# Order of the first loads and of the last units in a kernel of windowed attention and a gated MLP

## The chip, the cores and the metric

The kernel runs on one core of one Trainium2 chip. The time is that of the device in microseconds (us); shown is the median of several executions. One execution was also taken by the hardware profiler, and all times of single instructions are from it. The engines are named as in the profile: PE (TensorE, matmul), PEld (its weight loads), DVE (VectorE), ACT (ScalarE), POOL (GpSimd), and SP (SyncE, which issues most transfers). An engine works through its own instructions in the order in which they stand.

## The reference: what is computed

A sequence of 2048 rows of 512 numbers, x, is normalized to xn. One branch (A) is attention with 32 heads of 16 numbers over a window of 8 rows at distance 2; the other (B) is a layer norm, a mixing of neighbouring rows, and an MLP. Their product is added to x:

```python
xn = _layernorm(x, axis=-1)
s = _A_ref(xn, A_wqkv, A_wo)
g = _silu(_B_ref(xn, B_w1, B_w2, B_w3, B_w4))
return x + s * g
```

with, in short,

```python
# A: q, k, v from xn @ wqkv, heads of 16, row i sees rows i, i-2, ..., i-14
logits = jnp.einsum("bhsd,bhswd->bhsw", q, kg) * scale
...
o = jnp.einsum("bhsw,bhswd->bhsd", attn, vg)
return (lambda x, *d: x.transpose(*d))(o, 0, 2, 1, 3).reshape(B, S, D) @ wo
# B
h = _gelu(_layernorm(x, axis=-1) @ w1)
...
x1 = x + hs
h2 = _gelu(_layernorm(x1, axis=-1) @ w3) @ w4
return x1 + h2
```

## The kernel before, in words

**Tiling.** Since the window steps by two rows, even and odd rows never meet in the attention; the rows are split by parity p (0, 1), 1024 rows each. A tile of x is 128 rows of 512 numbers of one parity (bf16, 128 KB); four tiles make a chunk c (chunks 0 and 1 are parity 0, chunks 2 and 3 parity 1), and x tile j of chunk c is found by `x_tile(c, j)`. All data stay on the chip in arrays `xn`, `xnT` (turned), `kT`, `qT`, `oT`.

**Start.** SP issues the loads in the order of the code (lines 115 to 133): tiles 0 and 1 of chunk 0, the first half of the q/k weights as one transfer of 512 KB (`wqk_sb[:, :, 0:512]`, the q columns), tiles 2 and 3, the second half (the k columns), then chunks 1 and 2 in pairs of tiles, `w1`, and chunk 3. PE meanwhile makes ten matmuls on ones (L147). For tiles 0 and 1 DVE takes statistics (`stats`, L208 and L209), ACT the root (`root`, L217), DVE the inverse and the norm (L220, L224). `first_columns` (L290 to L293) turns both tiles on PE and copies half of the result by DVE and half by ACT. Then the same statistics, roots and norms follow for tiles 2 and 3 (lines 438 to 443). `qk(0, 0)` (L309) makes 32 matmuls of 256 columns for the first two tiles, in groups nt 0 to 7: groups 0 to 3 use the first half of the weights and 4 to 7 the second, and ahead of groups 6 and 7 PE turns tiles 2 and 3 (L264).

**Middle.** qk, w1, w2, w3 for all chunks. Each of these runs on PE with little else in its way.

**Units.** The attention goes in 17 units n (0 to 16; `NN = 17`): unit 0 holds the first rows of both parities, units 1 to 8 are parity 0, 9 to 16 parity 1, 120 query rows each. One turn n of the loop (lines 868 to 929) has the scores of unit n (L616), the weighted sum of unit n - 1 (L663), ACT's exp (L627), the values of the next unit (L595), one tile of the MLP's w4 product (L542), DVE's band mask (`within`, L636), and an output tile (`final`, L815). The weighted sum lies in `o_ps` and is taken out by DVE (L679, L680) and ACT (`evict`, L681) to `orw`; from there small transfers (`moves`, L706, one for each of 8 head groups) put the rows into `oT`. The softmax denominators of a run of units are gathered, inverted, written to DRAM and read back (L692, L770, L772, L778), and the result is multiplied into `oT` (`sums_apply`, L786). The last three runs (units 14, 15, 16; `R - 3` to `R - 1`) do this without DRAM: `sums_turn` (L716, PE), `sums_inverse` (L724 DVE; L729 ACT spreads the inverse over 16 columns), `sums_back` (L754, PE), `sums_mult` (L763, DVE). Units 15 and 16 also come to `oT` by `rows` (L741 PE, L746 ACT) and not by transfers.

**Output.** `final(p, i)` makes tile i of parity p: four matmuls with `wo`; then `gate(eng)`: DVE multiplies with the gate (L826, or L824 where the gate came by silu), and `eng` (mostly POOL) adds x (L831). `store` (L857) writes two tiles at a time. The gate of tile t is x1 + h2 (`w4_part`, DVE add at L550) through a tanh form of silu (L568, L574); for t = 14 and 15 (`NN - 3`, `NN - 2`) ACT's own silu is used (`gate_silu`, L560), for which L935 loads its table. For t = 15 PE adds x by an identity matmul (L548) and silu reads the matmul's result.

**What sets the order.** At the end (lines 977 to 984) every engine's instructions are tied to the order of the code. The order among the engines is found by a scheduler. It also hands out semaphores: transfers issued by SP and ACT get one of eight completion semaphores in turn, in the order in which the scheduler issues them.

Of the kernel before, what the change touches and what calls it, by code (L numbers as in the profile page):

```python
# [8 lines left out]
AF = mybir.ActivationFunctionType  # L9
ALU = mybir.AluOpType  # L10
# [5 lines left out]
def kernel(  # L16
# [68 lines left out]
    def smt(shape, name):  # L85
        return sm4.tile(shape, BF16, name=name, tag="s4")
# [25 lines left out]
    xn = [bigt([P, M // P, D], f"xn{p}") for p in range(2)]  # L112
    wqkv_v = A_wqkv.rearrange("(dt q) n -> q dt n", q=P)

    def load_x(c, n):
        p, k = c // 2, c % 2
        for t0 in range(k * TPC, (k + 1) * TPC, n):
            sp.dma_start(
                out=xn[p][:, t0 : t0 + n, :],
                in_=xv[p, t0 * P : (t0 + n) * P, :].rearrange("(i q) d -> q i d", q=P),  # L120
            )
            yield

    wqk_sb = midt([P, ND, 2 * D], "wqk_sb")
    first = load_x(0, 1)
    for k in range(2):
        next(first), next(first)
        sp.dma_start(out=wqk_sb[:, :, k * D : (k + 1) * D], in_=wqkv_v[:, :, k * D : (k + 1) * D])
    list(load_x(1, 2))
    list(load_x(2, 2))  # L130
    w1_sb = smt([P, ND, D], "w1_sb")
    sp.dma_start(out=w1_sb, in_=B_w1.rearrange("(dt q) n -> q dt n", q=P))
    list(load_x(3, 2))

    act.preload_act_table_set("sqrt_and_others")
    ident = const.tile([P, P], BF16, name="ident")
# [63 lines left out]
    def x_tile(c, j):  # L200
        return xn[c // 2][:, (c % 2) * TPC + j, :]

    def stats(c, j, key="l1"):
        if (key, c) not in mvs:
            mvs[key, c] = small.tile([P, TPC, nc.vector.BN_AGGR_DIM], F32, name=key + "m", tag=key + "m")
            rs[key, c] = small.tile([P, TPC], F32, name=key + "r", tag=key + "r")
        st = small.tile([P, nc.vector.BN_STATS_DIM], F32, name=key + "s", tag=key + "s")
        dve.bn_stats(out=st, in_=x_tile(c, j))  # L208
        dve.bn_aggr(out=mvs[key, c][:, j, :], in_=st)  # L209
# [6 lines left out]
    def root(c, a, b):  # L216
        act.activation(rs["l1", c][:, a:b], mvs["l1", c][:, a:b, 1], AF.Sqrt, bias=eps[:, 0:1])  # L217
# [211 lines left out]

    stats(0, 0)  # L430
    root(0, 0, 1)
    stats(0, 1)
    root(0, 1, 2)
    for j in range(2):
        inverse(0, j, j + 1)
        norm(0, j)
# [98 lines left out]
    def w4_part(t, lo, hi, tag="w"):  # L535
        c, jj = t // TPC, t % TPC
        if lo == 0:
            banks["w4", t] = pst(tag, "w4_ps")[:, 0, :]
        pt = banks["w4", t]
        for ft in range(lo, hi):  # L540
            fs = P if ft < NF - 1 else FL
            pe.matmul(  # L542
                pt, lhsT=h3[c][:fs, ft, jj * P : (jj + 1) * P], rhs=w4_sb[:fs, ft, :],
                start=(ft == 0), stop=(ft == NF - 1 and t < NN - 2),
            )
        x_i = x_tile(c, jj)
        if hi == NF and t == NN - 2:
            pe.matmul(pt, lhsT=ident[:], rhs=x_i, start=False, stop=True)  # L548
        elif hi == NF:
            dve.tensor_tensor(out=x_i, in0=pt, in1=x_i, op=ALU.add)  # L550
            gates.append(t)


    gates = []
    twice = set()

    def gate_silu(t):

        x_i = x_tile(t // TPC, t % TPC)
        act.activation(x_i, banks["w4", t] if t == NN - 2 else x_i, AF.Silu)  # L560
        twice.add(t)

    def gate_tanh():
# [74 lines left out]
    orw = {}  # L638
# [77 lines left out]
            pe.matmul(pt[0:QU, g, :], lhsT=w[:, g, :], rhs=ident[:, DH::32], start=True, stop=True)  # L716
        rden[i] = pt

    def sums_inverse(i, copy=lambda: None, behind=False):

        pt = rden[i]
        rb = small.tile([P, 2 * ND, 4], BF16, name="rbt", tag="rbt")
        with nc.allow_low_precision("bf16 weights"):
            dve.reciprocal(out=rb[0:QU], in_=pt[0:QU])  # L724
        if not behind:
            copy()
        rx = slot().rearrange("p (s j c d) -> p s j c d", s=ND, j=2, c=4)
        for j in range(2):
            act.activation(  # L729
                rx[0:QU, :, j], rb[0:QU, j * ND : (j + 1) * ND, :].unsqueeze(3).to_broadcast([QU, ND, 4, DH]), AF.Copy  # L730
            )
        if behind:
            copy()
        rden[i] = rx

    def rows(i, tag):

        pt = pst(tag, "row_ps")[:, 0, 0 : ND * QU].rearrange("p (s q) -> p s q", s=ND)
        for dt in range(ND):
            for jj in range(2):  # L740
                pe.matmul(  # L741
                    pt[P // 2 * jj : P // 2 * (jj + 1), dt, :], lhsT=heads, rhs=orw[i][:, ND * jj + dt, :],
                    start=True, stop=True, tile_position=(0, P // 2 * jj),
                )
        _, _, _, q0, rw, parts = run_of(runs[i][0])
        return lambda: act.activation(oT[parts[0][0]][:, :, q0 : q0 + rw], pt, AF.Copy)  # L746

# [108 lines left out]
    def store(q, p, i, n=2, cs=slice(0, D)):  # L856
        q.dma_start(  # L857
            out=ov[p, i * P : (i + n) * P, cs].rearrange("(i q) d -> q i d", q=P),
            in_=xo[p, i & ~1][:, i % 2 : i % 2 + n, cs],
        )  # L860
# [7 lines left out]
    for n in range(NN - 1):  # L868
        scores(n)
        back = [i for i, (a, b) in enumerate(runs) if b == n - 2 and i < R - NC]  # L870
        done = [i for i, (a, b) in enumerate(runs) if b == n - 1]
        evict = weighted(n - 1) if n > 0 else lambda: None
        for i in back:
            sums_invert(i)
        exps(n, 2 if n == 0 else 1)
        if n == NN - 2:
            values(n + 1)
        evict()
        if 0 < n < NN - 2:
            values(n + 1)  # L880
        gate_mult()
        if n < NN - 2:
            gate_tanh()
        for i in done:
            if i < R - NC:
                sums_gather(i)
        if n == 2:
            moves(0, [sp, pool], 1)
        for i in back:
            if 0 < i < R - NC - 1:  # L890
                moves(i, [sp], None, [6, 7])
            sums_read(i)
        for i in done:
            if i == 0:
                moves(i, [sp, pool], 0)
            elif i < R - NC - 1:
                moves(i, [pool, sp], None, range(6))
            elif i == R - NC - 1:
                moves(i, [pool], None, range(4))
            else:  # L900
                moves(i, [pool, sp])
        if n == NN - 2:
            store(sp, 0, 6)
        within(n, 2 if n == 0 else 1)
        late = [i for i, (a, b) in enumerate(runs) if n == max(b + 3, 5)]
        w4_part(n, 0, NF if n < NN - 2 else CUT)
        if n == 0:
            values(n + 1)
        gate = final(*final_at[n]) if n in final_at else None
        if n == NN - 2:  # L910
            banks["end"] = True
            sums_turn(R - 3, "o")
            sums_inverse(R - 3)
            for i in late:
                sums_apply(i)
        if gate:
            gate(pool)
        if n < NN - 2:
            for i in late:
                sums_apply(i)  # L920
        if n == NN - 3:
            moves(R - NC - 1, [pool], None, range(4, 8))
        if n % 2 == 0 and 10 <= n < NN - 3:
            load_xo((n - 2) // 8, (n - 2) % 8)
        if n - 1 in final_at and n % 2 == 0 and n < NN - 3:
            p, i = final_at[n - 1]
            store(sp, p, i - 1)
        if n in (10, 12):
            load_xo(1, n - 6)
    scores(NN - 1)  # L930
    evict = weighted(NN - 2)
    store(sp, 1, 0)
    exps(NN - 1)
    evict()
    act.preload_act_table_set("silu_and_others")  # L935
    w4_part(NN - 2, CUT, NF)
    gate_silu(NN - 2)
    within(NN - 1)
    gate2 = final(1, 2, "b")
    layout("high", f=1, g=1, h=1, i=1)  # L940
    sums_back(R - 3, "f")
    gate3 = final(1, 3, "h")
    sums_apply(R - 4, pool)
    evict = weighted(NN - 1, first=lambda: gate2(pool))
    evict()
    sums_turn(R - 2, "g")
    sums_inverse(R - 2, rows(R - 2, "i"), True)
    gate3(pool)
    store(sp, 1, 2)
    gate4 = final(1, 4, "w")  # L950
    sums_mult(R - 3)
    sums_turn(R - 1, "g")
    sums_back(R - 2, "f")
    sums_inverse(R - 1, rows(R - 1, "h"), True)
    sums_mult(R - 2)
    gate_silu(NN - 3)
    gate5 = final(1, 5, "b")
    gate4(pool)
    gate5(pool)
    store(sp, 1, 4)  # L960
    sums_back(R - 1, "i")
    gate6 = final(1, 6, "g")
    sums_mult(R - 1)
    halves = [slice(0, D // 2), slice(D // 2, D)]
    add6 = pe_add(1, 6, "o", slice(0, D))
    gate6(None)
# [48 lines left out]
```

## Time and profile before

| what | us |
|---|---|
| median of 3 runs (lowest, highest) | 198.9 (197.78, 199.8) |
| the profiled execution | 197.92 |
| its span, first to last instruction | 195.9 |
| PE busy in the span | 189.5 |
| ACT busy | 126.7 |
| DVE busy | 124.1 |
| POOL busy | 62.9 |
| DMA bytes in the span | 23.36 MB |
| first matmul of qk starts at | 6.73 |
| last scores (unit 16) start at | 180.13 |
| last projection (rows of parity 1, tile 7) starts at | 190.81 |

How to read the lines: in a timeline a row is start, duration, engine, line of the code, operation, output and inputs with their sizes, how many, and in brackets how long the engine had been idle before and what ended the wait. SPq, ACTq and POOLq are the issue of transfers by that engine; the row's duration is that of the issue and not of the transfer.

### The profile page before, as it was taken

The numbers are of one execution on the slowest core, as the hardware profiler recorded it, in microseconds if no ns is written. First come the engines' busy times: TensorE is split into PE (matmuls) and PEld (weight loads), VectorE is DVE, ScalarE is ACT, GpSimd is POOL, SyncE is SP. The second block draws the span as 40 slices with busy tenths as digits, with TensorE's granted clock in tenths as the row PEclk, the third lists the DMA queues.
The fourth block names the chain that finished last, engine by engine and source line by source line (L and its number), as shares of the span: only waits on it lengthen the run. The fifth ranks groups of instructions, "written<-read, shape, count | busy, mean of one in ns | idle before, by whom it ended". The sixth has DMA issues, their size and how long they took to land.

```text
span 195.9 us, 6180 instructions
## 1 busy us (share of the span) xinstructions
PE 189.5 (97%) x2607; PEld 100.7 (51%) x2607; DVE 124.1 (63%) x247; ACT 126.7 (65%) x140; POOL 62.9 (32%) x114
## 2 busy tenths in 40 slices
PE   7799999999999999999999999999999999999992
PEld 2688748644444444444445555555555545546551
DVE  4879885029359968200005677788778888886893
ACT  3579867836721534666558788887666666677971
POOL 4146738201301121100000623032625242469761
PEclk9999999999999999999999999999999999999999
DMA  5985265799660366350420012222233271723243
GB/s 149 330 270 137 77 144 161 141 300 357 185 155 3 107 157 162 113 107 0 155 84 0 14 25 65 76 48 67 44 97 67 56 210 27 234 39 87 70 141 109
DMA packets 36251, 23.36 MB, mean 119 GB/s; under 512 B 19680, under 2 KB 35712, under 8 KB 36224
## 3 DMA queue, kind: packets, MB, share of 16 engines
q1 hardware_dynamic: 34864, 22.11, 40.2%
q0 software_dynamic: 1216, 0.81, 2.1%
q8 instruction: 20, 0.33, 0.7%
q10 hardware_dynamic: 144, 0.07, 0.1%
q14 instruction: 7, 0.06, 0.1%
HBM read 12.41 MB, written 5.36 MB: 91 GB/s over the span
## 4 chain that ended last, share of the span: by engine, by line
PE 90%; DVE 4%; ACT 2%; DMA 1%; issue 1%; DVEq 0%
PE w_ps L542 19%; PE w_ps L406 18%; PE qk_ps L309 14%; PE v_ps L595 8%; PE w_ps L342 7%; PE w_ps L366 7%; PE wo_ps L815 5%; PE o_ps L663 5%; PE s_ps L616 3%; PE w_ps L422 1%; DMA xn<-in_A_x_dram 1%; ACT prob L627 1%; DVE prob L636 1%; PE tr_ps L264 1%; PE dt_ps L716 1%
## 5 line engine op out<-in xcount | busy, mean ns | idle before, releaser
L627 ACT ACTIVATE prob<-s_ps 128x2048 bf16<-128x2048 f32 (+1 forms) x18 | 31.9, 1780 | 17.9 <-PE s_ps L616 17.9
L542 PE MATMUL w_ps<-w_sb,h3T 128*128 128x512 bf16 (+1 forms) x176 | 40.8, 380 | 0.0
L410 ACT ACTIVATE h3T<-w_ps 128x1024 bf16<-128x1024 f32 x20 | 20.5, 1023 | 24.9 <-PE w_ps L406 24.9
L706 POOL DMA_DIRECT2D oT<-orw x38 | 19.4, 518 | 49.8 <-DVE orw L671 30.3
L406 PE MATMUL w_ps<-x1nT,w_sb 128*128 128x512 bf16 x160 | 35.0, 379 | 0.0
L309 PE MATMUL qk_ps<-xnT,wqk_sb 128*128 128x256 bf16 (+1 forms) x224 | 29.7, 288 | 0.5 <-DVE xnT L292 0.4
L542 PEld LDWEIGHTS <-h3T 128*128 128x128 bf16 (+1 forms) x176 | 17.0, 98 | 20.4
L309 PEld LDWEIGHTS <-wqk_sb 128*128 128x128 bf16 x224 | 21.5, 98 | 7.6 <-issue 0.8
L406 PEld LDWEIGHTS <-w_sb 128*128 128x128 bf16 x160 | 15.6, 98 | 19.1 <-issue 0.4
L636 DVE TENSOR_TENSOR prob<-prob,band 128x2048 bf16<-128x2048 bf16 (+1 forms) x18 | 21.3, 1183 | 2.4 <-ACT prob L627 2.3
L316 ACT ACTIVATE qT<-qk_ps,sel 128x1024 bf16<-128x1024 f32 x16 | 16.8, 1111 | 7.1 <-PE qk_ps L309 7.0
L831 POOL TENSOR_TENSOR xo<-sg,xo 128x512 bf16<-128x512 bf16 x9 | 11.7, 1305 | 21.6 <-DVE sg L826 21.6
L371 DVE TENSOR_TENSOR xn<-w_ps,xn 128x1024 bf16<-128x1024 f32 x8 | 9.7, 1212 | 13.2 <-PE w_ps L366 13.2
L815 PE MATMUL wo_ps<-wo_sb,oT 128*128 128x512 bf16 (+1 forms) x68 | 16.6, 367 | 0.1
L595 PE MATMUL v_ps<-wv_sb,xnT 128*128 128x512 bf16 x64 | 16.6, 382 | 0.0
L550 DVE TENSOR_TENSOR xn<-w_ps,xn 128x512 bf16<-128x512 f32 x15 | 10.4, 690 | 7.5 <-PE w_ps L542 7.5
L598 DVE CAST v_aug<-v_ps 128x512 bf16<-128x512 f32 x1 | 0.7, 691 | 22.5 <-ACT h3T L410 22.5
L681 ACT ACTIVATE orw<-o_ps 128x896 bf16<-128x896 f32 x16 | 14.6, 913 | 0.4 <-PE dt_ps L716 0.4
L366 PE MATMUL w_ps<-w_sb,hT 128*128 128x512 bf16 x64 | 14.3, 379 | 0.0
L342 PE MATMUL w_ps<-xn2T,w_sb 128*128 128x512 bf16 x64 | 14.3, 379 | 0.0
L213 POOL TENSOR_SCALAR l3r<-l3m 128x4 f32<-128x4 f32 x4 | 1.8, 451 | 36.9 <-DVE l3m L209 36.9
L663 PE MATMUL o_ps<-prob,v_aug 64*32 64x64 bf16 x1088 | 12.2, 196 | 0.3 <-DVE prob L636 0.2
(100 smaller groups left out, 240.1 us busy)
## 6 DMA issues: line engine op xcount, KB each, us to landing
x1n_dram<-xn SPq DMA_DIRECT2D x4, 512.0 KB
xn<-in_A_x_dram SPq DMA_DIRECT2D x6, 256.0 KB
xo<-in_A_x_dram SPq DMA_DIRECT2D x6, 256.0 KB
out_dram<-xo SPq DMA_DIRECT2D x6, 256.0 KB
orw<-rden_d SPq DMA_DIRECT2D x6, 240.0 KB
w_sb<-in_B_w_dram SPq DMA_DIRECT2D x1, 1376.0 KB
w_sb<-in_B_w_dram SPq DMA_DIRECT2D x1, 1280.0 KB
wqk_sb<-in_A_wqkv_dram SPq DMA_DIRECT2D x2, 512.0 KB
```

Source lines behind the costliest of these rows:

```text
L309: pe.matmul(pt[:, b, :], lhsT=wqk_sb[:, dt, nt * P : (nt + 1) * P], rhs=xnT[p][:, dt, ms], start=(dt == 0), stop=(dt == ND - 1),)
L342: pe.matmul(pt[:, b, :], lhsT=w1_sb[:, dt, g * P : (g + 1) * P], rhs=xn2T[:, dt, :], start=(dt == 0), stop=(dt == ND - 1),)
L366: pe.matmul(pt[:, j, :], lhsT=w2_src(p, g, m0), rhs=w2_sb[:, g, :], start=(g == 0), stop=(g == ND - 1),)
L406: pe.matmul(pt[:, b, :], lhsT=w3_sb[:, dt, ft * P : (ft + 1) * P], rhs=x1nT[:, dt, :], start=(dt == 0), stop=(dt == ND - 1),)
L410: act.activation(h3_tile(c)[:, 2 * a : 2 * a + 2, :], pt, AF.Gelu_apprx_tanh)
L542: pe.matmul(pt, lhsT=h3[c][:fs, ft, jj * P : (jj + 1) * P], rhs=w4_sb[:fs, ft, :], start=(ft == 0), stop=(ft == NF - 1 and t < NN - 2),)
L595: pe.matmul(vp, lhsT=xnT[p][:, dt, k0 : k0 + P], rhs=wv_sb[:, dt, :], start=first, stop=last)
L627: act.activation(pr[:, rs_], t[:, rs_], AF.Exp, scale=SCALE)
L636: dve.tensor_tensor(out=w, in0=w, in1=b.unsqueeze(1).to_broadcast([P, m, KB]), op=ALU.min)
L663: pe.matmul(op[32 * cg : 32 * cg + 32, s, g * KB : (g + 1) * KB], lhsT=va[KB * s : KB * s + KB, dt * 8 + h, :], rhs=pr[KB * s : KB * s + K ...
L706: queues[hh % len(queues)].dma_start(out=oT[p][DH * hh : DH * (hh + 1), :, q0 : q0 + nq], in_=w[32 * cg : 32 * cg + DH, ND * jj : ND * jj ...
L815: pe.matmul(pt, lhsT=oT[p][:, dt, i * P : (i + 1) * P], rhs=wo_sb[:, dt, cs], start=(dt == 0), stop=(dt == ND - 1),)
```

## The change

At the start, `load_x` now loads n tiles from tile j on, on a queue that is given, and `load_qk(k)` loads half k of the q/k weights as four transfers of 128 KB, one for each 128 rows of the matrix. SP issues tiles 0 and 1 and the first half ahead of the rest; x tiles 2 and 3 are issued by ACT, one after each of the first two roots; SP's next ones in the code are the second half, chunks 1 and 2, w1, chunk 3.

At the end, for units 14 to 16 and their outputs: unit 14's eight moves go three to SP (issued ahead of the reading of unit 13's sums) and five to POOL, and not in turn to both; `sums_inverse` hands back its ACT part as `spread`, which is called later (for unit 14 after the exp of unit 16 and the eviction of unit 15); `gate(None)` multiplies tile (1, 1) ahead of `sums_apply`, and its add on POOL comes after unit 13's `sums_apply`; `w4_add` on DVE takes the place of the identity matmul for t = 15, whose silu moves behind that of t = 14; `sums_back` of unit 14 and the gates of tiles (1, 2), (1, 3) and (1, 4) change places; `rows` uses 2 matmuls of 480 columns where it had 8 of 120.

```diff
+    def load_x(c, j, n=1, queue=sp):
+        p, t0 = c // 2, c % 2 * TPC + j
+        queue.dma_start(
+            out=xn[p][:, t0 : t0 + n, :], in_=xv[p, t0 * P : (t0 + n) * P, :].rearrange("(i q) d -> q i d", q=P)
+        )
+
+    def load_qk(k):
+        for dt in range(ND):
+            sp.dma_start(out=wqk_sb[:, dt, k * D : (k + 1) * D], in_=wqkv_v[:, dt, k * D : (k + 1) * D])
...
-    first = load_x(0, 1)
-    for k in range(2):
-        next(first), next(first)
-        sp.dma_start(out=wqk_sb[:, :, k * D : (k + 1) * D], in_=wqkv_v[:, :, k * D : (k + 1) * D])
-    list(load_x(1, 2))
-    list(load_x(2, 2))
...
+    for j in range(2):
+        load_x(0, j)
+    load_qk(0)
...
     root(0, 0, 1)
+    load_x(0, 2, 1, act)
     stats(0, 1)
     root(0, 1, 2)
+    load_x(0, 3, 1, act)
+    load_qk(1)
+    for c in (1, 2, 3):
+        if c == 3:
+            w1_sb = smt([P, ND, D], "w1_sb")
+            sp.dma_start(out=w1_sb, in_=B_w1.rearrange("(dt q) n -> q dt n", q=P))
+        for j in (0, 2):
+            load_x(c, j, 2)
...
-        x_i = x_tile(c, jj)
-        if hi == NF and t == NN - 2:
-            pe.matmul(pt, lhsT=ident[:], rhs=x_i, start=False, stop=True)
-        elif hi == NF:
-            dve.tensor_tensor(out=x_i, in0=pt, in1=x_i, op=ALU.add)
-            gates.append(t)
+        if hi == NF and t < NN - 2:
+            w4_add(t)
...
-        for dt in range(ND):
-            for jj in range(2):
-                pe.matmul(
-                    pt[P // 2 * jj : P // 2 * (jj + 1), dt, :], lhsT=heads, rhs=orw[i][:, ND * jj + dt, :],
...
+        for jj in range(2):
+            pe.matmul(
+                pt[P // 2 * jj : P // 2 * (jj + 1)], lhsT=heads, rhs=orw[i][:, ND * jj : ND * (jj + 1), :],
...
+        if n == NN - 2:
+            moves(R - 3, [sp], None, range(3))
...
-                moves(i, [pool, sp])
+                moves(i, [pool], None, range(3, 8))
...
             sums_turn(R - 3, "o")
-            sums_inverse(R - 3)
+            spread14 = sums_inverse(R - 3)
+            gate(None)
             for i in late:
                 sums_apply(i)
-        if gate:
+        elif gate:
             gate(pool)
...
     evict = weighted(NN - 2)
-    store(sp, 1, 0)
     exps(NN - 1)
     evict()
+    spread14()
     act.preload_act_table_set("silu_and_others")
     w4_part(NN - 2, CUT, NF)
-    gate_silu(NN - 2)
     within(NN - 1)
+    w4_add(NN - 2)
     gate2 = final(1, 2, "b")
     layout("high", f=1, g=1, h=1, i=1)
-    sums_back(R - 3, "f")
     gate3 = final(1, 3, "h")
     sums_apply(R - 4, pool)
-    evict = weighted(NN - 1, first=lambda: gate2(pool))
+    gate.add(pool)
+    store(sp, 1, 0)
+    gate2(pool)
+    evict = weighted(NN - 1)
     evict()
     sums_turn(R - 2, "g")
-    sums_inverse(R - 2, rows(R - 2, "i"), True)
+    spread15 = sums_inverse(R - 2)
+    copy15 = rows(R - 2, "i")
+    sums_back(R - 3, "f")
     gate3(pool)
     store(sp, 1, 2)
+    spread15()
+    copy15()
     gate4 = final(1, 4, "w")
     sums_mult(R - 3)
+    gate4(pool)
     sums_turn(R - 1, "g")
     sums_back(R - 2, "f")
-    sums_inverse(R - 1, rows(R - 1, "h"), True)
+    spread16 = sums_inverse(R - 1)
+    copy16 = rows(R - 1, "h")
+    spread16()
+    copy16()
     sums_mult(R - 2)
     gate_silu(NN - 3)
+    gate_silu(NN - 2)
     gate5 = final(1, 5, "b")
-    gate4(pool)
     gate5(pool)
+    sums_back(R - 1, "i")
+    sums_mult(R - 1)
     store(sp, 1, 4)
-    sums_back(R - 1, "i")
     gate6 = final(1, 6, "g")
-    sums_mult(R - 1)
```

More of the change, by code (lines that the diff above doesn't have):

```diff
@@ L113 @@
     wqkv_v = A_wqkv.rearrange("(dt q) n -> q dt n", q=P)
[L115 to L122, printed above, removed]
-    wqk_sb = midt([P, ND, 2 * D], "wqk_sb")
-    first = load_x(0, 1)
-    for k in range(2):
-        next(first), next(first)
-        sp.dma_start(out=wqk_sb[:, :, k * D : (k + 1) * D], in_=wqkv_v[:, :, k * D : (k + 1) * D])
-    list(load_x(1, 2))
-    list(load_x(2, 2))
-    w1_sb = smt([P, ND, D], "w1_sb")
-    sp.dma_start(out=w1_sb, in_=B_w1.rearrange("(dt q) n -> q dt n", q=P))
-    list(load_x(3, 2))
+    def load_x(c, j, n=1, queue=sp):
[6 more added lines that the diff above has]
+            sp.dma_start(out=wqk_sb[:, dt, k * D : (k + 1) * D], in_=wqkv_v[:, dt, k * D : (k + 1) * D])
+    wqk_sb = midt([P, ND, 2 * D], "wqk_sb")
+    for j in range(2):
+        load_x(0, j)
+    load_qk(0)
     act.preload_act_table_set("sqrt_and_others")
@@ L543, in w4_part, with w4_add @@
                 pt, lhsT=h3[c][:fs, ft, jj * P : (jj + 1) * P], rhs=w4_sb[:fs, ft, :],
-                start=(ft == 0), stop=(ft == NF - 1 and t < NN - 2),
+                start=(ft == 0), stop=(ft == NF - 1),
             )
-        x_i = x_tile(c, jj)
-        if hi == NF and t == NN - 2:
-            pe.matmul(pt, lhsT=ident[:], rhs=x_i, start=False, stop=True)
-        elif hi == NF:
-            dve.tensor_tensor(out=x_i, in0=pt, in1=x_i, op=ALU.add)
-            gates.append(t)
+        if hi == NF and t < NN - 2:
+            w4_add(t)
+    def w4_add(t):
+        x_i = x_tile(t // TPC, t % TPC)
+        dve.tensor_tensor(out=x_i, in0=banks.pop(("w4", t)), in1=x_i, op=ALU.add)
+        gates.append(t)
     gates = []
@@ L559, in gate_silu @@
         x_i = x_tile(t // TPC, t % TPC)
-        act.activation(x_i, banks["w4", t] if t == NN - 2 else x_i, AF.Silu)
+        act.activation(x_i, x_i, AF.Silu)
         twice.add(t)
@@ L717, in sums_turn, with sums_inverse @@
         rden[i] = pt
-    def sums_inverse(i, copy=lambda: None, behind=False):
+    def sums_inverse(i):
         pt = rden[i]
@@ L724, in sums_inverse, with spread @@
             dve.reciprocal(out=rb[0:QU], in_=pt[0:QU])
-        if not behind:
-            copy()
         rx = slot().rearrange("p (s j c d) -> p s j c d", s=ND, j=2, c=4)
[L728 to L733, printed above, removed]
-        rden[i] = rx
+        rden[i] = rx
+        def spread():
+            for j in range(2):
+                act.activation(
+                    rx[0:QU, :, j], rb[0:QU, j * ND : (j + 1) * ND, :].unsqueeze(3).to_broadcast([QU, ND, 4, DH]),
+                    AF.Copy,
+                )
+        return spread
     def rows(i, tag):
         pt = pst(tag, "row_ps")[:, 0, 0 : ND * QU].rearrange("p (s q) -> p s q", s=ND)
-        for dt in range(ND):
-            for jj in range(2):
-                pe.matmul(
-                    pt[P // 2 * jj : P // 2 * (jj + 1), dt, :], lhsT=heads, rhs=orw[i][:, ND * jj + dt, :],
-                    start=True, stop=True, tile_position=(0, P // 2 * jj),
-                )
+        for jj in range(2):
+            pe.matmul(
+                pt[P // 2 * jj : P // 2 * (jj + 1)], lhsT=heads, rhs=orw[i][:, ND * jj : ND * (jj + 1), :],
+                start=True, stop=True, tile_position=(0, P // 2 * jj),
+            )
         _, _, _, q0, rw, parts = run_of(runs[i][0])
```

## The prediction

> **What bounds the kernel now.** I read the page first, then the timeline of the first 22 us, then the timeline of the last 31 us, and last the waits and the chain.
>
> ```profile
> span 195.9 us, 6180 instructions
> ...
> PE 189.5 (97%) x2607; PEld 100.7 (51%) x2607; DVE 124.1 (63%) x247; ACT 126.7 (65%) x140; POOL 62.9 (32%) x114
> ...
> PE 90%; DVE 4%; ACT 2%; DMA 1%; issue 1%; DVEq 0%
> ```
>
> TensorE (PE) is busy for 97% of the span and makes 90% of the chain that ended last. Between the first qk matmul at 6.73 us and about 180 us the chain is nearly all PE, so nothing there hides a late start: what the first qk matmul loses is lost at the end, and only the first 7 and the last 16 us can be changed by this edit. The start:
>
> ```profile
> 0.80 0.88 SPq L118 DMA_DIRECT2D xn<-in_A_x_dram  x2
> ...
> 1.11 3.67 PE L147 MATMUL warm_ps<-ones_bf 128*128 128x512 bf16 x10 [1.11 <-DVE ones_bf L139]
> ...
> 1.72 0.43 SPq L128 DMA_DIRECT2D wqk_sb<-in_A_wqkv_dram  x1
> ...
> 2.19 0.98 SPq L118 DMA_DIRECT2D xn<-in_A_x_dram  x2
> ...
> 3.15 0.69 DVE L208 BATCH_NORM_STATS2 l1s<-xn 128x6 f32<-128x512 bf16 x1 [1.41 <-DMA xn<-in_A_x_dram]
> ...
> 4.89 0.29 ACT L217 ACTIVATE l1r<-l1m,eps 128x1 f32<-128x1 f32 x1 [0.50 <-DVE l1r L220]
> ...
> 6.59 0.68 DVE L208 BATCH_NORM_STATS2 l1s<-xn 128x6 f32<-128x512 bf16 x1
> ...
> 6.73 2.94 PE L309 MATMUL qk_ps<-xnT,wqk_sb 128*128 128x256 bf16 x24 [0.40 <-DVE xnT L292]
> ...
> 8.62 0.77 PEld L309 LDWEIGHTS <-wqk_sb 128*128 128x128 bf16 x8 [0.20 <-DMA wqk_sb<-in_A_wqkv_dram]
> ```
>
> To be seen: an x tile issued at 0.80 is there at 3.15 (2.35 us); tile 1's root (ACT, 4.89) leads in 1.84 us to the first qk matmul; tiles 2 and 3 are there before DVE asks at 6.59; the second half of the weights is the one late transfer (0.20 us). The end:
>
> ```profile
> 180.63 0.72 ACT L729 ACTIVATE slots<-rbt 120x256 bf16<-120x256 bf16 x2 [1.38 <-DVE rbt L724]
> ...
> 181.25 1.86 ACT L627 ACTIVATE prob<-s_ps 128x2048 bf16<-128x2048 f32 x1
> ...
> 183.14 1.68 DVE L636 TENSOR_TENSOR prob<-prob,band 128x2048 bf16<-128x2048 bf16 x1 [0.25 <-ACT prob L627]
> ...
> 184.28 1.49 POOL L786 TENSOR_TENSOR oT<-oT,orw 128x480 bf16<-128x480 bf16 x1 [0.54 <-DMA orw<-rden_d]
> ...
> 184.87 0.68 PE L663 MATMUL o_ps<-prob,v_aug 64*32 64x64 bf16 x64 [0.20 <-DVE prob L636]
> ...
> 189.66 2.26 POOL L831 TENSOR_TENSOR slots<-slots 128x512 bf16<-128x512 bf16 x2 [1.40 <-PE wo_ps L815]
> ...
> 191.95 1.41 SPq L857 DMA_DIRECT2D out_dram<-slots  x3
> ```
>
> Unit 16 (the last) goes scores, exp, band (DVE), weighted sum, and the exp stands behind unit 14's spread on ACT.
>
> **The change at the start.** The built program tells more than the diff. Transfers of SP and ACT share eight completion semaphores, handed out in the scheduler's own order of issue, and a transfer that reuses one first waits for its former user to land. The scheduler places all SP's loads ahead of ACT's two. So in the built program tile 2's load waits for the eighth SP transfer (piece 1 of the second weight half) and tile 3's for the ninth (piece 2). They are not the seventh and eighth. ACT works in order: behind tile 2's load stand tile 1's root, tile 3's load, half of the first columns' copy (L293), and the roots of tiles 2 and 3; DVE's inverse and norm of tile 1 wait for that root, and PE's transposes for them.
>
> When does the eighth transfer land? By issue: SP took 0.44 us each for two x tiles, 0.43 for half the weights, 0.51 each for four x loads (3.69, 2.04 us); at 0.47 the eighth starts at 0.80 + 7 x 0.47 = 4.1, and with 2.35 us of flight lands at 6.45; at 0.41, the shortest in the start, 6.0. By bytes: before, 1.5 MB had landed at 8.62; the eighth transfer ends 1.0 MB, and 0.5 MB less at the 350 GB/s of the 8 to 10 us window is 1.5 us, so 7.1. The late end is the whole second half without tiles 2 and 3 ahead of it (256 KB, 0.7 us): 7.9. I take 6.7, between the two nearest.
>
> ACT then issues for 0.39 us (its one issue, the last store), so the root runs at 7.1 instead of 4.89: **+2.2 us**. Tile 3's load goes at 7.4 to 7.8, before the copy behind it is due (6.37 + 2.2). Tiles 2 and 3 land 2.35 us after their issue, at 9.05 and 9.75. DVE wants them at 6.59 + 2.2 = 8.8 and, 0.86 us of statistics later, at 9.9, so tile 3's norm ends at 9.9 + 1.9 = 11.8, and its transposes are due at 10.17 + 2.2 = 12.4: 0.6 us of cover. The 0.20 us wait for weights goes, since all pieces are there by about 8 and wanted after 11. Splitting the weights costs SP six more issues (2.8 us) less two x issues (0.98); the x loads behind them start 1.8 us later, and chunk 1's first tile, wanted before at 9.36, is now wanted at 11.6: nothing. Start: **+2.0**, bounds +1.3 - 0.2 = +1.1 and 7.9 + 0.39 - 4.89 - 0.2 = +3.2.
>
> One price hangs on the PE's own clock. Its ten warm-up matmuls take 620 ns in the median and 379 at best, which is the length that later groups of 512 columns have: PE begins at about half pace. Before, 1.9 us with eight transposes lay between warm-up and qk, and 24 matmuls of 256 columns took 2.94 us, near the later pace (64 in 6.99). After, this gap is 4.8 to about 8.9. I leave it out of the sum: the four transposes of tile 0 stay at 5.4 in its middle. The Trainium skill, TensorE: Matmul & The Clock Gate, Part 1, says that an idle window of about 3.4 us puts PE back to half rate and that the window runs free of the kernel. By that rule the sum would sometimes be that of the half-pace rival below; no run so far shows such a gap.
>
> **The change at the end.** (a) The spread of unit 14 moves behind ACT's exp and eviction: the exp starts when the scores are done (180.56) instead of at 181.25, 0.6 us sooner, and ends at 182.5. (b) The add of rows (1,1) on POOL moves behind L786, away from the band step, which took 1.68 us beside it and 1.21 in its earlier turns: band ends at about 183.75 instead of 184.83. (c) PE loses the identity matmul (0.22 us) and puts unit 14's turn-back (0.21) after the last weighted sum, so it arrives at 184.05 and no longer waits: **-0.8 us** there. (d) ACT: exp to 182.5, eviction 0.91, spread 0.72, table load 1.28, so the eviction of unit 16 starts at 185.45 instead of 186.20. (e) DVE gets the w4 add (0.69) and the product (1,2) ahead of unit 16's parts; from 183.75 its list is 0.69 + 0.68 + 0.23 + 0.23 + 0.36 + 0.63 + 0.65 + 0.68, with overlaps of some 0.1 each, so unit 16's reciprocal comes at 187.5 instead of 187.83. (f) From there PE's list gives the last projection at 190.0 instead of 190.81. The row matmuls, 8 to 2 with as many columns, lie beside PE's waits. (g) POOL: L786 to 185.77, then five adds of 1.15, to 191.5 instead of 191.92; the three last stores (1.41) end at 192.9 instead of 193.36. Unit 14's moves: three on SP (0.65 each from 179.3, done 181.2, just before the read of unit 13's sums at 181.34), five on POOL (0.5 each, done 182.2, POOL idle till 184.28): nothing. If they go at the 0.88 of the pair at 175.34, the read and L786 come 0.55 later, and most of the gain goes. End: **-0.65**, between PE's -0.8 and the stores' -0.45; bounds -0.85 and, with the late read and DVE's longer list, +0.2.
>
> **Sum.** +2.0 - 0.65 = +1.35. The profiled execution took 197.92 us (span 195.9 and 2.0 around it), 1.0 below the median of the runs shown. So 199.3 for such an execution, and 198.9 + 1.35 = **200.3** as a median.
>
> **Rivals.**
> *Slower, by PE at half pace*: if the gap lets PE's clock fall, the first qk matmuls run at half pace for about the 2.7 us (1.11 to 3.9) that the warm-up needed, which costs 1.35 us: 201.6. It decides where PE has no work for long enough between 4.8 and 8.9. For it: the half-pace warm-up; against: the eight transposes, four in the middle.
> *Slower, by late weights*: the eighth transfer lands at 7.9, because ACT's loads and small pieces slow each other: start +3.2, 201.5. The DMA engines are full from 4 us on, which speaks for it; that 0.5 MB less is ahead, against.
> *The loads really go as seventh and eighth* (no wait): issued at 4.4 and 5.2, there at 6.75 and 7.6, the root in time at 4.89, tile 3 late by less than its cover; -0.2 - 0.65: 198.1. The built program speaks against it.
> *The end gains nothing*: 198.9 + 2.0 = 200.9, or a little more.
>
> **How the numbers follow.** Forecast 0.55, with its own range 199.3 to 201.2; half pace 0.17; late weights 0.10; no wait 0.13; lost end 0.05. About 1% (2.0 us) is what a measurement of this kernel can tell from no change, so above 200.9 is slower: both slow rivals, 0.09 of the forecast's upper part, and some of the lost end, 0.38. Faster, under 196.9, needs no wait and more at the end than its bound: 0.03. The rest, 0.59, is no change. The range runs from 198.7 (part of the no-wait case left out) to 202.0.
>
> **What would show it.** In the new profile: tile 1's root (ACT) at about 7.1, with ACT idle before tile 2's load; the first qk matmul at about 8.9; the weights' wait at 8.62 gone; statistics of tile 2 starting near 9. Then the whole middle later by the same 2.0 us. At the end, in times less that shift: exp at 180.6, band of 1.2 us, no PE wait before the last weighted sum, five adds on POOL in a row after L786. The prediction is wrong if the root still runs near 4.9, if the first 24 qk matmuls take over 4 us, or if the end, counted from the last scores to the last store, is not shorter.

## The result, and the profile after

The changed kernel takes 205.03 us (median of 6 runs, 204.19 to 208.09) beside 198.69 us before (6 runs): a ratio of 1.031, interval 1.028 to 1.034. Measured once more, in another job, it took 205.67 (204.84 to 207.37) beside 198.26: 1.038, 1.034 to 1.042. It is slower by 6 to 7 us, where 1.35 us were forecast and 202.0 was the upper end of the range. The profiled execution took 207.6 us, one of two runs out of six that lay 2.5 us or more above the median with a lower granted clock; a second profile of the same kernel took 206.6, and where the two differ both are given.

The start in the timeline of the changed kernel (columns as before: start, duration, engine, what, and in brackets the idle time before it with what ended it):

```profile
1.72 3.75 SPq L123 DMA_DIRECT2D wqk_sb<-in_A_wqkv_dram  x8
...
5.51 1.97 SPq L117 DMA_DIRECT2D xn<-in_A_x_dram  x4
7.03 0.38 ACTq L117 DMA_DIRECT2D xn<-in_A_x_dram  x1
7.47 0.29 ACT L212 ACTIVATE l1r<-l1m,eps 128x1 f32<-128x1 f32 x1 [3.15 <-DMA wqk_sb<-in_A_wqkv_dram]
7.52 0.47 SPq L435 DMA_DIRECT2D w_sb<-in_B_w_dram  x1
...
8.84 0.34 ACTq L117 DMA_DIRECT2D xn<-in_A_x_dram  x1
...
9.26 4.24 PE L304 MATMUL qk_ps<-xnT,wqk_sb 128*128 128x256 bf16 x24 [0.36 <-DMA xn<-in_A_x_dram]
...
12.27 0.69 DVE L203 BATCH_NORM_STATS2 l1s<-xn 128x6 f32<-128x512 bf16 x1 [3.06 <-DMA xn<-in_A_x_dram]
...
15.07 0.69 DVE L203 BATCH_NORM_STATS2 l1s<-xn 128x6 f32<-128x512 bf16 x1 [1.89 <-DMA xn<-in_A_x_dram]
...
16.54 0.61 PE L259 MATMUL tr_ps<-ident,xn 128*128 128x128 bf16 x4 [3.04 <-DVE xn L219]
...
18.22 5.24 PE L304 MATMUL qk_ps<-xnT,wqk_sb 128*128 128x256 bf16 x28
```

To be seen: ACT's load of tile 2 goes out at 7.03 and tile 2 is there at 12.27, 5.2 us later; tile 3's goes at 8.84 and is there at 15.07, 6.2 us later. (An x tile counts as there when DVE begins its statistics after waiting for it.) PE turns tile 2 at 16.54, where it did so at 9.51 before:

```profile
9.51 0.39 PE L264 MATMUL tr_ps<-ident,xn 128*128 128x128 bf16 x4
```

The chain that ended last runs through the same transfers:

```profile
4.56 4.26 DMA wqk_sb<-in_A_wqkv_dram
...
8.84 6.21 DMA xn<-in_A_x_dram
...
15.07 0.71 DVE l1s L203
```

The first row is the ninth SP transfer, for which tile 3's load waits until 8.82; the second is that load's own flight. The table by stages of 4 us has, for each window, its length, the busy time and count of PE, PEld, DVE, ACT and POOL, then PE's granted clock, the DMA share and GB/s:

```profile
8.00:12.00 4.00, 3.16 (x17) 2.05 (x18) 0.83 (x2) 0.60 (x1) 0.00 (x0) 0.59 0.92 283
12.00:16.00 4.00, 1.50 (x13) 1.08 (x11) 1.77 (x5) 0.29 (x1) 0.00 (x0) 0.93 0.85 282
16.00:20.00 4.00, 3.46 (x21) 2.73 (x22) 3.22 (x11) 2.98 (x4) 1.68 (x4) 0.50 0.00 1
```

PE's clock is 0.59 while the first qk matmuls run (24 in 4.24 us; 2.94 before) and 0.50 after the wait for tiles 2 and 3 (28 in 5.24 us; 3.57 before). Before, all these windows had 1.00.

The end:

```profile
188.95 2.67 SPq L710 DMA_DIRECT2D oT<-orw  x3
...
189.71 0.43 PE L620 MATMUL s_ps<-qT,kT 32*64 32x128 bf16 x32
...
190.30 1.88 ACT L631 ACTIVATE prob<-s_ps 128x2048 bf16<-128x2048 f32 x1 [1.38 <-PE s_ps L620]
...
191.85 0.64 SPq L782 DMA_DIRECT2D orw<-rden_d  x1
...
192.21 1.23 DVE L640 TENSOR_TENSOR prob<-prob,band 128x2048 bf16<-128x2048 bf16 x1 [0.49 <-ACT prob L631]
...
193.75 0.68 PE L667 MATMUL o_ps<-prob,v_aug 64*32 64x64 bf16 x64
...
194.91 1.09 POOL L790 TENSOR_TENSOR oT<-oT,orw 128x480 bf16<-128x480 bf16 x1 [3.12 <-DMA orw<-rden_d]
...
196.06 1.04 PE L819 MATMUL wo_ps<-wo_sb,oT 128*128 128x512 bf16 x3 [0.45 <-POOL oT L790]
...
202.46 0.38 ACTq L861 DMA_DIRECT2D out_dram<-slots  x1
```

Unit 16's scores start 9.58 us later than before (189.71, 180.13), and from them to ACT's store, the last issue, it is 12.75 us as before (12.77). The weighted sum comes 4.04 us after the scores (4.74 before), but unit 13's sums are read 2.14 us after them (1.21 before), and POOL's product with them (L790) starts 5.20 us after them (4.15 before). PE waits 0.45 us for it. Before, the read stood ahead of SP's moves:

```profile
181.34 0.65 SPq L778 DMA_DIRECT2D orw<-rden_d  x1
182.03 2.60 SPq L706 DMA_DIRECT2D oT<-orw  x4
```

So the two profiles differ by 2.5 us up to the first qk matmul (9.26 for 6.73), 4.5 more up to the turning of tile 2 (16.54 for 9.51), 2.4 more up to w1 (32.33 for 22.93), and nothing at the end. In the second profile of the changed kernel tiles 2 and 3 are there at 13.54 and 14.99, tile 2 is turned at 16.46 and w1 starts at 31.11: the last step is 1.2 us there.

### The profile page after: what moved, and what is told of

Read it like the earlier page. It is cut to its first block, busy times and chain, and to the rows that moved or that the text cites. A ratio compares the mean times of both kernels' runs of the same rounds, so it can differ in the third digit from the quotient of the medians.

```text
span 205.8 us, 6140 instructions
## 1 busy us (share of the span) xinstructions
PE 192.4 (93%) x2569; PEld 102.9 (50%) x2594; DVE 124.4 (60%) x248; ACT 126.5 (61%) x140; POOL 62.7 (30%) x115
## 4 chain that ended last, share of the span: by engine, by line
PE 79%; DMA 10%; SPq 2%; ACT 2%; POOL 2%; issue 2%; DVE 1%; POOLq 0%; ACTq 0%; DVEq 0%
PE w_ps L401 17%; PE w_ps L546 15%; PE qk_ps L304 14%; PE w_ps L361 7%; PE w_ps L337 7%; PE v_ps L599 6%; PE wo_ps L819 5%; PE o_ps L667 4%; DMA oT<-orw 3%; DMA xn<-in_A_x_dram 3%; PE s_ps L620 2%; DMA wqk_sb<-in_A_wqkv_dram 2%; DMA orw<-rden_d 1%; PE w_ps L417 1%; SPq L123 1%
## 5 line engine op out<-in xcount | busy, mean ns | idle before, releaser
L710 POOL DMA_DIRECT2D oT<-orw x39 | 19.9, 518 | 49.9 <-DVE orw L675 30.3
L304 PE MATMUL qk_ps<-xnT,wqk_sb 128*128 128x256 bf16 (+1 forms) x223 | 33.1, 311 | 0.4 <-DMA xn<-in_A_x_dram 0.4
L304 PEld LDWEIGHTS <-wqk_sb 128*128 128x128 bf16 x224 | 23.5, 107 | 8.9 <-DMA xn<-in_A_x_dram 0.5
L640 DVE TENSOR_TENSOR prob<-prob,band 128x2048 bf16<-128x2048 bf16 (+1 forms) x18 | 20.8, 1158 | 2.8 <-ACT prob L631 2.8
L599 PE MATMUL v_ps<-wv_sb,xnT 128*128 128x512 bf16 x49 | 15.8, 382 | 0.8
L555 DVE TENSOR_TENSOR xn<-w_ps,xn 128x512 bf16<-128x512 f32 x16 | 11.0, 690 | 7.9 <-PE w_ps L546 7.8
L203 DVE BATCH_NORM_STATS2 l1s<-xn 128x6 f32<-128x512 bf16 x16 | 10.8, 673 | 6.3 <-DMA xn<-in_A_x_dram 6.3
```

The costliest lines, as they stand in the source:

```text
L304: pe.matmul(pt[:, b, :], lhsT=wqk_sb[:, dt, nt * P : (nt + 1) * P], rhs=xnT[p][:, dt, ms], start=(dt == 0), stop=(dt == ND - 1),)
L599: pe.matmul(vp, lhsT=xnT[p][:, dt, k0 : k0 + P], rhs=wv_sb[:, dt, :], start=first, stop=last)
L640: dve.tensor_tensor(out=w, in0=w, in1=b.unsqueeze(1).to_broadcast([P, m, KB]), op=ALU.min)
L710: queues[hh % len(queues)].dma_start(out=oT[p][DH * hh : DH * (hh + 1), :, q0 : q0 + nq], in_=w[32 * cg : 32 * cg + DH, ND * jj : ND * jj ...
```

## The experiments

Each was measured beside the kernel before in its own job; differences are from that job's median. Twelve runs were made.

**The start alone.** The new loads, with the end of before.

> The start of the change alone, with the old end. Theory A: the whole loss comes from the two x tiles on ScalarE's queue, which wait for the eighth and ninth transfer and then travel over 5 us beside SyncE's backlog of 256 KB loads, and the end gains nothing: 205.0, within 0.7. Rival, the end gained the forecast 0.65 and hid part of the loss: 205.7. Rival, the end costs several us: 201 or less. Tiles 2 and 3 are there at about 12.3 and 15.1 us of the span.

Measured 206.27 (ratio 1.040, 1.034 to 1.047), +7.7 us. The start carries the whole loss, and more than was expected of it (205.0, within 0.7). In its profile tile 2's statistics run at 14.18, 6.5 us after ACT's issue at 7.65.

**The end alone.** The old loads, with the end of the change.

> The end of the change alone, with the old loads. Theory A: 198.7, within 0.4, because the exp moves 0.6 us ahead but the read of unit 13's sums comes about 0.9 us later behind three moves on SyncE, so the last projection keeps its distance from the last scores (10.7 us). Rival, the forecast: 198.0. Rival, the end is what is slow: 201 or more.

Measured 198.55 (0.9995, 0.996 to 1.003): nothing, as the theory had it. Its timeline shows what takes the gain:

```profile
179.84 3.36 SPq L706 DMA_DIRECT2D oT<-orw  x3
180.59 0.27 PEld L616 LDWEIGHTS <-kT 32*64 32x64 bf16 x32
...
183.42 0.64 SPq L778 DMA_DIRECT2D orw<-rden_d  x1
...
186.60 1.09 POOL L786 TENSOR_TENSOR oT<-oT,orw 128x480 bf16<-128x480 bf16 x1 [3.93 <-DMA orw<-rden_d]
...
187.75 1.04 PE L815 MATMUL wo_ps<-wo_sb,oT 128*128 128x512 bf16 x3 [1.10 <-POOL oT L786]
```

The three moves of unit 14 take 1.12 us each on SP, the read stands behind them, POOL waits 3.93 us for the read, and PE 1.10 us for POOL. The order of the waits is what these rows show, not their usual size: the profiled run is the longest of the ten (200.33), and its end takes 15.03 us (scores 180.59, ACT's store 195.62). After PE's wait the granted clock falls to 0.50 there (190 to 192), and four matmuls of 512 columns take 1.89 us for 1.04. In the two profiles of the changed kernel the same waits make no such fall, and the end takes 12.75 and 12.95.

**The end with the read first.** The old loads; SP's three moves are issued behind the read:

```diff
-        if n == NN - 2:
-            moves(R - 3, [sp], None, range(3))
...
             sums_read(i)
+        if n == NN - 2:
+            moves(R - 3, [sp], None, range(3))
```

> The old loads with the new end, and the three moves on SyncE behind the read of unit 13's sums. Theory A, that read is what took the end's gain: POOL's product starts about 4.2 us after the last scores (5.2 in the change), the last projection 10.0 after them (10.7), total 0.5 to 0.7 below the kernel before, 198.0. Rival, VectorE's longer list or the adds on POOL hold the end as well: 198.5.

```profile
181.36 0.43 PE L616 MATMUL s_ps<-qT,kT 32*64 32x128 bf16 x32
...
182.71 0.65 SPq L778 DMA_DIRECT2D orw<-rden_d  x1
183.42 1.96 SPq L706 DMA_DIRECT2D oT<-orw  x3
...
185.81 1.10 POOL L786 TENSOR_TENSOR oT<-oT,orw 128x480 bf16<-128x480 bf16 x1 [2.36 <-DMA orw<-rden_d]
...
193.48 0.40 ACTq L857 DMA_DIRECT2D out_dram<-slots  x1
```

Measured 197.73 (12 runs; 0.9975, 0.9954 to 0.9996): 0.7 us faster than before and the fastest kernel of this study, by a small margin. From scores to ACT's store it is 12.12 us, 0.65 less than before: the forecast of the end, with one order changed. Behind the read the moves take 0.65 us each.

**The pieces alone.** The loads of before, in their order, with each half of the q/k weights in four transfers.

> The kernel before with one edit: each half of the q/k weights in four pieces; tiles 2 and 3 stay on SyncE between the halves. Theory A, order and queue matter and not the size: the tiles there at about 7.0 and 7.4, their norms covered by the first 24 qk matmuls, 198.7, within 0.5. Rival, small pieces are slow in themselves: 200 or more.

```profile
9.61 0.28 PE L310 MATMUL qk_ps<-xnT,wqk_sb 128*128 128x256 bf16 x1 [0.77 <-DMA wqk_sb<-in_A_wqkv_dram]
10.49 0.72 PE L310 MATMUL qk_ps<-xnT,wqk_sb 128*128 128x256 bf16 x5 [0.60 <-DMA wqk_sb<-in_A_wqkv_dram]
```

Measured 199.48 (1.006, 1.004 to 1.008), +1.0 us: the theory missed, and so did the rival's 200. Six more issues make the last pieces late: the last is issued by 6.41, where the second half was out by 3.64. PE waits 1.4 us for them where it waited 0.20 before (and 0.47 and 0.86 in the profiles of the end alone and of the read first, which have the old loads). The bytes come more slowly too. From 4 to 8 us the three profiles with halves in one transfer move 329 to 336 GB/s, and six with pieces (this one, one queue, the start alone, the change filled, the changed kernel twice) 220 to 246. One piece per 0.47 us is 279 GB/s at most, so pieces are not free on a queue that issues at this pace.

**The same loads on one queue.** The start of the change, but SP issues tiles 2 and 3, behind the eight pieces.

> The start of the change with the old end, but SyncE itself issues tiles 2 and 3, behind the eight weight pieces: ScalarE's root of tile 1 waits for nothing. Theory A: tiles there at about 7.5 and 7.9, first qk matmul at 6.7, tile 3's norm about 0.5 us later than before and mostly covered: 198.9. Rival, small weight pieces are themselves slow: 200 or more.

```profile
4.76 0.29 ACT L212 ACTIVATE l1r<-l1m,eps 128x1 f32<-128x1 f32 x1 [0.50 <-DVE l1r L215]
...
8.90 0.70 DVE L203 BATCH_NORM_STATS2 l1s<-xn 128x6 f32<-128x512 bf16 x1 [2.36 <-DMA xn<-in_A_x_dram]
...
11.16 0.40 PE L259 MATMUL tr_ps<-ident,xn 128*128 128x128 bf16 x4 [1.72 <-DVE xn L219]
```

Measured 200.22 (1.009, 1.006 to 1.012), +1.7. Tile 1's root is in time, no load stands on ACT, and still tile 2, issued at 5.51, takes 3.4 us. The theory's 198.9 fell, the rival's 200 or more held.

**ACT issues tiles 2 and 3 first of all.**

> The start of the change with the old end, but ScalarE issues tiles 2 and 3 first of all, with semaphores not used before: no wait, and the whole backlog of SyncE beside and behind them. Theory A, backlog ahead of a load makes it slow, and there is none yet: tiles there by about 5, the root of tile 1 at 5, first qk matmul at about 7, total 198.7 to 199.2. Rival, a load on ScalarE's queue loses against SyncE's whenever both have work: tiles after 8 and 200 or more.

Measured 199.03 (1.005, 1.001 to 1.009), +0.6, in the theory's range. ACT's queue is not slow in itself: its loads, issued from 0.79, never make DVE wait, and the profile's count of packets by queue has all 288 of them through by 3.8 us. What is left is that tile 0, on SP's queue beside them, comes at 3.78 instead of 3.15.

**The wait without the backlog.** ACT's two loads wait for the same two weight pieces, by a copy of one column of each; SP's loads of chunks 1 to 3 and w1 go only when tile 1 is normalized:

```diff
+    act.activation(look[0], wqk_sb[:, 1, D : D + 1], AF.Copy)
     load_x(0, 2, 1, act)
...
+    dve.tensor_copy(out=x_tile(1, 0)[:, 0:1], in_=x_tile(0, 1)[:, 0:1])
     for c in (1, 2, 3):
```

> The start of the change with the old end; ScalarE's two loads still wait for the same two weight pieces (a copy of one column of each ahead of the load), but SyncE's loads of chunks 1 to 3 are held until tile 1 is normalized (a one-column copy into their destination). Theory A, the backlog makes the loads slow: each takes 2.3 to 3 us, tiles 2 and 3 are there at about 9.7 and 10.4, 24 qk matmuls from about 9.3, total 200.7. Rival, a load on ScalarE's queue takes 5 us whatever runs beside it: 204 to 205. Rival, PE's clock falls in the gap up to 9.3 in any case: 202.

```profile
7.58 0.38 ACTq L117 DMA_DIRECT2D xn<-in_A_x_dram  x1
8.01 0.29 ACT L212 ACTIVATE l1r<-l1m,eps 128x1 f32<-128x1 f32 x1 [0.23 <-issue]
8.06 0.38 ACTq L117 DMA_DIRECT2D xn<-in_A_x_dram  x1
...
9.90 0.69 DVE L203 BATCH_NORM_STATS2 l1s<-xn 128x6 f32<-128x512 bf16 x1
9.91 3.89 PE L304 MATMUL qk_ps<-xnT,wqk_sb 128*128 128x256 bf16 x24 [0.30 <-DMA xn<-in_A_x_dram]
```

Measured 202.71 (1.021, 1.015 to 1.028), +4.2. The two loads now take at most 2.3 us and DVE does not wait for them: what the theory said of the backlog held. Its time, 200.7, did not: the root at 8.01 shifts qk to 9.91, and the 24 matmuls take 3.89 us for 2.94, the falling clock of the expectation's rival (202). The granted clock is 0.70 from 8 to 10 us and 0.50 from 10 to 12.

**Neither wait nor backlog.** As the last one, without the copies; ACT's loads wait only for the first two weight pieces.

> The new start alone, with neither the wait nor the backlog: ACT's loads of tiles 2 and 3 wait only for the first two weight pieces, which land near 4 us, and SP issues the x loads of the next chunks and w1 only when tile 1 is normalized. Old end. With the run that has the wait alone (202.71) and the one with both (206.27) it splits the loss. Theory (a load on ACT's queue lands 2.3 us after its issue when SP has little outstanding, and the backlog makes the rest of the 5 to 6 us): tile 2's load goes near 4.5, tile 1's root near 5.2, tile 2's statistics run at 7 to 8 with no more than 1 us of waiting, the clock holds, time 199.2 to 200.2. Rival (ACT's loads are slow while SP's eight weight pieces are still landing, whatever stands behind them): tiles 2 and 3 at 9 or later, and 201 or more.

```profile
4.36 0.38 ACTq L117 DMA_DIRECT2D xn<-in_A_x_dram  x1
4.86 0.29 ACT L212 ACTIVATE l1r<-l1m,eps 128x1 f32<-128x1 f32 x1 [0.50 <-DVE l1r L215]
...
6.70 2.45 PE L304 MATMUL qk_ps<-xnT,wqk_sb 128*128 128x256 bf16 x19 [0.40 <-DMA xn<-in_A_x_dram]
8.40 0.69 DVE L203 BATCH_NORM_STATS2 l1s<-xn 128x6 f32<-128x512 bf16 x1 [1.75 <-DMA xn<-in_A_x_dram]
```

Measured 199.65 (1.006, 1.003 to 1.009), +1.4, within the theory's range. But DVE waits 1.75 us and not 1 at most: tile 2 takes 4.0 us behind the weight pieces that are under way (and, from 6.06 on, beside SP's next x loads).

The medians of these kernels, from two jobs, split the start: +1.4 for pieces and order, +2.8 for the wait on ACT (4.2 less 1.4), +3.5 for the backlog (7.7 less 4.2). The last two hold what PE loses at half pace in them.

**PE kept busy, in the whole change.** 12 matmuls of 512 columns are added before tile 1's transposes and 36 of 256 before the turning of tile 2; nothing reads them.

> The change whole, with 12 matmuls of 512 columns on ones ahead of tile 1's transposes and 36 of 256 columns ahead of tile 2's; their results are overwritten. Theory A, half pace is a price of its own: all 128 qk matmuls after 17 us at full pace, granted clock 1.0, and 2 to 3 us less than the change, about 202.5. Rival, the clock costs nothing beside the waits: 205, within 0.7.

```profile
9.52 2.84 PE L310 MATMUL qk_ps<-xnT,wqk_sb 128*128 128x256 bf16 x24 [0.40 <-DMA xn<-in_A_x_dram]
...
15.67 0.69 DVE L203 BATCH_NORM_STATS2 l1s<-xn 128x6 f32<-128x512 bf16 x1 [1.79 <-DMA xn<-in_A_x_dram]
...
17.13 0.40 PE L259 MATMUL tr_ps<-ident,xn 128*128 128x128 bf16 x4 [0.84 <-DVE xn L219]
```

Measured 205.7 (4 runs; 1.036, 1.030 to 1.041), no better than the changed kernel, as the rival had it. The clock stays at 1.00, the matmuls have their full pace, and from the turning of tile 2 to w1 it is 13.51 us (15.79 and 14.65 in the changed kernel's two profiles); but tile 3 is there 0.6 us later. PE at full pace has the same tiles to wait for.

**PE kept busy, in the wait without the backlog.** Sixteen such matmuls before tile 1's transposes.

> The run with the wait alone (202.71), with sixteen matmuls of 512 columns added between tile 0's and tile 1's transposes, so that PE has no gap from 5 to 9 us; they write the warm-up's bank, and nothing reads them. If PE's half pace is what that run lost beyond its wait: the 24 qk matmuls in 2.85 instead of 3.89 us, and 201.4 to 201.9. Rival (the half pace is covered by other waits there, as in the whole change): 202.5 or more.

```profile
9.89 0.39 PE L290 MATMUL tr_ps<-ident,xn 128*128 128x128 bf16 x4
...
10.68 2.84 PE L309 MATMUL qk_ps<-xnT,wqk_sb 128*128 128x256 bf16 x24 [0.40 <-DVE xnT L292]
```

Measured 201.48 (1.016, 1.013 to 1.019). It lies in the theory's range, but its interval overlaps that of the kernel without the filling, so this is inconclusive. The trace says why the gain is small: the matmuls are 1.05 us shorter (2.84 for 3.89), but the filling ran until 10 us and delayed qk by 0.77 (10.68 for 9.91).

**The whole change with the read first.**

> The whole change, with unit 14's three moves on SP placed behind the read of unit 13's sums. Theory (the end gains 0.65 us once the read isn't behind the moves, also after the new start): 0.6 to 0.8 us less than the changed kernel in the same job, so about 204.4 where that takes 205.0; scores of unit 16 to the last store 12.1 instead of 12.75. Rival (the late start sets the end too, by another clock phase): no difference.

Measured 204.67 (1.029, 1.025 to 1.033) beside 205.67 (1.038, 1.034 to 1.042) for the unaltered change in the same job. In its trace the end is 12.13 us long (scores 188.03, ACT's store 200.16), in that of the unaltered change 12.95 (188.50, 201.45). The gain of the end holds after the new start too; the medians' 1.0 us is more than the trace's 0.8, and the intervals only just part.

**The changed kernel again**, as the measure for the last ones:

> The changed kernel once more, unaltered, as the measure for the other three in the same job: 205.0 within 0.7, as before.

It took 205.67, as told above.

## Why the prediction was wrong, point by point

**"Tiles 2 and 3 land 2.35 us after their issue, at 9.05 and 9.75": this step failed.** They came after 5.2 and 6.2 us (6.2 and 7.2 in the second profile). The 2.35 us was read from tile 0's load, which goes out with nothing ahead of it. How much was ahead in the other cases can be estimated from the issues so far and the GB/s of the windows up to then. The profile also counts the packets of each queue: a tile's load is 144 packets, and where ACT issues it, they have a queue of their own. "First packets" is the first 0.2 us in which that queue moves more than 5:

| load | issued | ahead of it, not yet moved | first packets | there | flight |
|---|---|---|---|---|---|
| tile 2, wait without backlog | 7.58 | 1.31 MB - 172 GB/s x 7.58 = 0.0 MB | 8.8 | by 9.90 | 2.3 |
| tile 2, one queue | 5.51 | 1.31 - 155 x 5.51 = 0.5 MB | SP's queue | 8.90 | 3.4 |
| tile 2, neither | 4.36 | 1.05 - 132 x 4.36 = 0.5 MB | 6.0 | 8.40 | 4.0 |
| tile 2, changed kernel | 7.03 | 2.10 to 2.36 - 175 x 7.03 = 0.9 to 1.1 MB | 10.2 | 12.27 | 5.2 |
| tile 2, its second profile | 7.33 | 2.36 - 177 x 7.33 = 1.1 MB | 10.8 | 13.54 | 6.2 |
| tile 3, changed kernel | 8.84 | 3.02 - 183 x 8.84 = 1.4 MB | 12.6 | 15.07 | 6.2 |
| tile 2, start alone | 7.65 | 2.88 - 170 x 7.65 = 1.6 MB | 11.6 | 14.18 | 6.5 |

By this estimate the flight is about 2.3 us and 2.4 to 3.7 us more for each MB that was issued earlier, on whichever queue. Most of the addition passes before the first packet: 1.2 us after the issue with nothing ahead, 3.2 to 4.0 us in the last four rows. Between 7.03 and 10.0 in the changed kernel SP's queue moves 0.69 MB and ACT's nothing. ACT's packets begin when all but 0.1 to 0.5 MB of what SP had issued earlier has moved; the rest of the addition falls in the time in which both queues move. The changed kernel lets SP issue its x loads of chunk 1 and 2 at 5.51, before ACT's.

The prediction had both halves of this, DMA engines full from 4 us on and a flight of 2.35 us with them empty, and did not put them together. It used the full engines only for the eighth transfer. There its two reckonings gave 6.45 (by issue) and 7.1 (by bytes), and 7.0 and 7.3 were measured. The 350 GB/s of the second (the row has 360) were those of the old loads; the changed loads brought 225 and 234 from 4 to 8 us.

The Trainium skill, DMA: Bandwidth & Descriptors, section Queues, rings and completion order, says that each DMA engine goes round its queues, a packet from one and then from the next. Where both queues move, this trace agrees: from 10.4 to 11.0 us ACT's queue moves 82 packets and SP's 81. That share comes too late to help, since the load has stood for 3.2 us by then. What holds its first packets back is open: the runs show that it goes with what SP issued earlier, and not by which step.

**Tile 3 "at 7.4 to 7.8": half right.** Its load, waiting for the ninth SP transfer, went at 8.84 in one profile and at 7.78 in the other, and tile 3 was there at 15.07 and 14.99. In these two profiles an issue a microsecond earlier brought nothing.

**"The root runs at 7.1 instead of 4.89: +2.2 us": right.** It ran at 7.47 and 7.76, and qk started 2.5 and 2.8 us later. The wait that ends at the eighth transfer stands in the rows: ACT is idle for 3.15 us up to that root, for `wqk_sb`. (The lower bound of that term, with the eighth transfer at 6.0, comes to 6.0 + 0.39 - 4.89 - 0.2 = +1.3 and not +1.1; nothing hangs on it.)

**"0.6 us of cover" for tile 3's norm: too little by far.** With tiles at 12.3 and 15.1, PE stood for 3.04 us before 16.54.

**"Splitting the weights ... nothing": wrong on its own terms.** Pieces alone cost 1.0 us in the old order, as later issues and fewer GB/s. In the changed order PE waits for no weights, as forecast, but the six added issues and the eight pieces under way are what tile 2 waits behind in the kernel with neither wait nor backlog.

**PE at half pace, a rival with 0.17: it came true, beside the failed step.** The windows show 0.59 and 0.50. At the first 24 matmuls, where the rival had it, the wait for the late tiles covers the price. Behind tile 3, after a second gap (3.04 and 2.40 us), it costs 2.4 and 1.2 us in the two traces, more than the 1.35 of the rival in one profile, less in the other. The rule of the Trainium skill that stood beside that rival (TensorE: Matmul & The Clock Gate, Part 1) agrees as to the fall. Here PE stood still for a little less than that rule's idle window, 2.74 us before 8.46, with 0.40 us of transposes ahead of it at 5.33; whether transposes count as work there, no run separates. Whether the half pace counts in the median stays open: the two fillings do not separate it from the loads.

**The end, -0.65: failed by its own stated condition.** "If they go at the 0.88 of the pair at 175.34" was the case: 0.89 us for each of SP's three moves in the changed kernel, 1.12 with the old loads. Exp, band and weighted sum moved as forecast (the last by 0.70), and the late read took it all: counted from the scores it came 0.93 us later than before, and POOL's product 1.05, where 0.55 had been named. With the read first the 0.65 is there. The row that gave 0.65 us a move (182.03) stood where POOL issued nothing.

**The sum.** In the first profiled execution: +2.5 (forecast +2.2), +4.5 for the late tiles (forecast none), +2.4 at half pace (forecast none, a rival), end 0 (forecast -0.65): +9.4, and 207.6 less 197.92 is 9.7. The medians differ by 6.3 and 7.4; the loads' landing and the clock vary from run to run.

## What to carry to other kernels

A transfer's flight is read from a row like its own: count what has been issued earlier and not yet moved, on all queues, and add its time to the flight on empty engines. An urgent load goes ahead of the bulk in time of issue; here another queue did not carry it past. Count also what splitting a transfer adds in issues. When a list of transfers is put ahead of a read that others wait for, the read pays for all of them, at the pace that they have beside the other issuing engines.

## What the runs showed of the hardware

- In these runs a load on ACT's queue hardly passes what SP issued earlier: 2.3 us of flight with nothing ahead, 5.2 to 6.5 us with 0.9 to 1.6 MB ahead (the table above; the MB are estimates). Its first packets move 1.2 us after the issue with nothing ahead and 3.2 to 4.0 us after it with that backlog. Once they move, the two queues share: 82 packets of ACT's and 81 of SP's from 10.4 to 11.0 us of the changed kernel, 135 and 169 from 12.8 to 13.6 in the start alone.
- From 4 to 8 us the loads move 329 to 336 GB/s with two transfers of 512 KB (three profiles) and 220 to 246 with eight of 128 KB (six profiles), at one issue per 0.47 us.
- SP's issue of a `moves` transfer takes 0.65 us when POOL issues none (183.42, 1.96 us for three) and 0.89 to 1.12 beside POOL's own (2.67 and 3.36 us for three).
- In the five profiles in which PE waited 2.7 to 3.2 us before tile 1's transposes (the changed kernel twice, the same with the read first, the start alone, the wait without the backlog), the 24 qk matmuls took 3.89 to 4.79 us, the four transposes at about 5.3 in the gap notwithstanding. With the gap filled they took 2.84, before 2.94.
- A granted clock of 1.00 does not prove full pace. It reads 1.00 in the warm-up, where ten matmuls of 512 columns take 4.45 us (four later ones take 1.03), and from 8 to 16 us of the whole change with the read first, where the 24 qk matmuls take 4.79.
